# Retention, a gated feed-forward and eight experts on one core: two more weight sets made ahead, two more jobs in seven-block form

## The chip, the core and the metric

The kernel runs on one core of one Trainium2 chip, as one launch. The metric is the device time of that launch in microseconds (us). Of the kernel before there are three timed runs: 1972.39, 1973.30 and 1973.48 us, median 1973.3 us.

## The reference, cut to what matters

All arithmetic is fp32. With N = 2304 tokens, model width 512:

```
# 1 retention: 4 batches x 8 heads, 576 positions, head width 64
scores = (q @ k.T) / sqrt(64);  ret = scores * gamma[h] ** (i - j) for i >= j, else 0
x = (ret @ v), heads joined                                  # 2304 x 512
# 2 gated feed-forward, width 1536
xn = x / sqrt(mean(x*x, -1) + 1e-6) * rms_g
x  = (silu(xn @ w_gate) * (xn @ w_val)) @ w_out
# 3 eight experts, width 1024 each
logits = x @ w_gate2;  P = exp(logits - max)
8 times: P /= P.sum(1) + 1e-9;  P /= P.sum(0) + 1e-9;  P *= N / E
out = sum over e of P[:, e] * (relu(x @ w1[e]) @ w2[e])
```

## The kernel before, in words

**Numbers in two parts.** TensorE multiplies fp32 values as pairs: each operand is split into a high part (a cast, on ACT) and a low part (value minus high, on VectorE, called DVE here, or on GpSimd, called POOL), and a product is three matmuls, high x high, high x low and low x high.

**Gated sweeps.** The feed-forward runs in six sweeps (numbered 0 to 5 here), each over 256 of the 1536 columns and over five blocks of tokens (512, 512, 512, 384, 384). `gated_block` (L203 to L256) does one block of one sweep. For each of two column tiles it makes a gate and a value product (TensorE, tiles `gv`), takes silu (ACT, tile `t`), multiplies (DVE, L221), casts the high part (ACT, `ghi`, L226) and subtracts the low part (DVE, `glo`, L227). The two halves then go through `w_out` (TensorE, tiles `x`), and the four results are added to `acc` (DVE, L250). The code is written as generators. Each block has five steps, and the `x` products of a block stand in the third step of the next block, behind that block's first gate and value products.

After each step two helpers put their own instructions into the same queues. `step_weights` narrows the next sweep's weights from 64-bit words to fp32 and splits them (DVE L137 to L143 and L159). `late_steps`, the second, makes expert weights ahead of time. Its program is `late_weights` and `late_plan` (L721 to L764): a list `PREPARED` of weight sets is spread evenly over 125 steps, from the last two blocks of sweep 0 to the third block of sweep 5. One set is 128 x 1024 raw values of `w1` or of `w2` for one job. `prepared` (L679 to L718) turns it into seven split blocks, in five pieces of work at the step numbers p, p+1, p+2, p+4 and p+5 (`LATE_PLACES`): ACT casts, DVE subtracts and stores on SyncE's queue (SP); four subtractions on POOL (L708), which make the sums that seven-block products need; ACT casts again; DVE subtracts again, stores, and SP's request of the raw tile for the third set after this one (three raw tiles, `ahead_raw`, rotate).

**Jobs.** The experts run as 96 jobs: three units of 768 tokens, in each eight experts, in each four pairs of 128-wide column tiles. The first product, x @ w1, is in seven-block form everywhere: a 2 x 2 by 2 x 2 block product made with seven block products instead of eight, and with sums and differences of blocks. The second product, h @ w2, has two forms. In the first `LATE` jobs (0 to 11) `outputs_of` (L946) makes it plainly: six token tiles, 36 matmuls of 512 columns. The same jobs prepare their own weights (`first_weights`, `second_weights`) and store them in DRAM (`w1_kept`, `w2_kept`) for the units after. From job `LATE` on the second product is in seven-block form as well: 42 matmuls of 384 columns, one job later than its first product. Job `LATE` is called the opening job: it ends the plain form of the job before it and starts the new one, and its sums lie in borrowed tiles (`opening_homes`), one of them the buffer `prob_b1`. The weights of jobs 12 to 31 are the ones that the sweeps made ahead; `load_w1` (L976) and `load_w2` request them from DRAM.

**What sets the order.** Each engine runs its instructions in the order in which the Python code issues them, and so does SP's queue, where a request waits until its source or its target is free. There is no scheduler. Two more names: `keep_probs` (L981) transposes four token tiles of the routing probabilities on TensorE, copies them on ACT into the single buffer `xs`, and stores them in DRAM (`prob_kept`); `load_probs` brings an expert's row back, spread over all partitions. `finish_unit` (L1222) transposes a unit's sums on TensorE, one PSUM bank after another, and stores the output.

Of the kernel before, what the change touches and what calls it, by code (L numbers as in the profile page):

```python
# [19 lines left out]
NT = B * S  # L20
DM = H * D
# [25 lines left out]
NU = NT // UNIT  # L47
NCH = UNIT // 128
NPAIR = FE // 256
UJ = E * NPAIR  # L50
ROUTED = NPAIR + 2
LATE = 12
LATE_PLACES = (0, 1, 2, 4, 5)
W2_TURN = (2 - LATE) % 3
PREPARED = [(1, 0)] + [(n, which) for n in range(LATE, UJ) for which in range(2)]
# [4 lines left out]
def retention_glu_experts(ctx: ExitStack, tc: tile.TileContext, a, out):  # L60
# [916 lines left out]
    def load_w1(n):  # L977
        if n < len(jobs):
            nc.sync.dma_start(f32(w1_slots[n % 2]).rearrange("p a b c -> p (a b c)"), w1_kept[n % UJ])

    def keep_probs(i):  # L981
        ps = pac.tile([E, 512], F32, tag="ac", name=f"pt{i}")
        tiles = range(4 * i, min(4 * i + 4, TT))
        for c, t in enumerate(tiles):
            nc.tensor.transpose(ps[:, c * 128:(c + 1) * 128], prob[:, t, :], ident)
        size = len(tiles) * 128
        st = ev.tile([128, 2, T], F32, tag="xs", name=f"pts{i}").rearrange("p a b -> p (a b)")[:E, :size]
        nc.scalar.copy(st, ps[:, :size])
        nc.sync.dma_start(prob_kept[:, i * 512:i * 512 + size], st)
# [3 lines left out]
    def load_probs(n):  # L993
        if n < len(jobs):
            u, e, _ = jobs[n]
            nc.sync.dma_start(prob_b[(e - LATE // NPAIR) % 2], prob_kept[e, u * UNIT:(u + 1) * UNIT].partition_broadcast(128))

# [14 lines left out]
    for n, (u, e, g) in enumerate(jobs[:LATE]):  # L1012
# [87 lines left out]
            for _ in ys:  # L1100
                pass
        ys = outputs_of(n)
        if ROUTED < n <= ROUTED + -(-NT // 512):
            keep_probs(n - ROUTED - 1)
    for _ in seconds:
        pass

# [44 lines left out]
    def low(n, i, engine=None):  # L1152
        (hi, lo), x = operand(n, i)
        (engine or nc.vector).tensor_sub(lo, x, f32(hi))  # L1154
# [28 lines left out]
    def shared(n, j):  # L1183
        second(n, j, S1, T1, shared_sums[j], start=begins_sum(n))
# [60 lines left out]
    for n, (u, e, g) in list(enumerate(jobs))[LATE:]:  # L1245
        opening = n == LATE
        m, l = n - 1, n - 2
        pb = prob_b[(e - LATE // NPAIR) % 2]
        load_w1(n + 1)
        if u + 1 < NU and (e, g) == (E - 1, NPAIR - 3):  # L1250
            switch = unit_operands(u + 1)
        ahead = u + 1 < NU and (e, g) in ((E - 1, NPAIR - 3), (E - 1, NPAIR - 2))
        turn = u + 1 < NU and (e, g) == (E - 1, NPAIR - 1)
        begins = n % UJ == 0
        h_blocks, sums = opening_homes if opening else homes
        if g == NPAIR - 1:
            load_probs(n + 1)

        block_product(n, px, 0, "A11", start=True)
# [15 lines left out]
        if opening:  # L1275
            block_product(n, pv, 3, "S1", start=True)
            nc.scalar.copy(p5, pv)
            next(ys)
            block_product(n, py, 4, "S2")
            nc.scalar.copy(pz, py)  # L1280
            next(ys)
        else:
            low(m, S2)
            low(m, A12)
            if l < LATE:
                block_product(n, qz, 3, "S1", start=True)
            block_product(n, py, 4, "S2")
            nc.scalar.copy(pz, py)
            if turn:
                next(switch)  # L1290
            first(m, 0)
            high(m, S4)
            low(m, S3, nc.gpsimd)
            low(m, S4, nc.gpsimd)
            shared(m, 0)
            if l >= LATE:
                block_product(n, qz, 3, "S1", start=True)
            nc.scalar.copy(p5, qz)
            if ahead or begins:
                next(switch)  # L1300
            third(m, 0)
            c11(m, 0)
            add_11(m, 0)
            if l >= LATE and jobs[l][1:] == (E - 1, NPAIR - 1):
                add_shared(jobs[l][0], 1)
# [64 lines left out]
    n, l = len(jobs) - 1, len(jobs) - 2  # L1370
# [29 lines left out]
        ev.tile([128, 2, T], F32, tag="xs", name="st_xs").rearrange("p a b -> p (a b)"), old[:, 3].rearrange("p h t -> p (h t)"),  # L1400
        prob_b[0], o_first[:, 1, :], z.rearrange("p h t -> p (h t)"), prob_b[1],
    ]
    for _ in finish_unit(NU - 1, [shared_all, px_all, qx_all, py_all, qy_all, shared_1], [t[:, :DM] for t in stages]):
        pass


# [74 lines left out]
```

## Time and profile before

| what | value |
|---|---|
| median of three runs | 1973.3 us |
| the profiled execution, its own time | 1973.84 us |
| its span, first to last instruction | 1972.1 us |
| busy TensorE / DVE / ACT / POOL | 1959.8 / 1556.0 / 944.2 / 867.9 us |
| granted TensorE clock | 1.00 throughout |
| DMA | 515.48 MB, mean 261 GB/s |

"Busy" is the time in which at least one instruction of an engine ran. The end of a matmul is modelled, so matmuls overlap in the rows: the distance between two starts tells more of TensorE than the length of one. In a timeline row the first number is the start, the second the length, and a bracket gives the idle time of the engine before the row and what ended it. In a row of waits the numbers are the total, how often, and the longest. The sweeps with weights made ahead lie between 131 and 503 us, the jobs from 529.5 us to the end.

### The profile page before, as it was taken

How to read it: one execution, taken by the hardware profiler on the slowest of the kernel's cores; microseconds unless marked ns; L12 is line 12 of the kernel's file. 1: busy time of each engine (PE TensorE's matmuls, PEld its weight loads, DVE VectorE, ACT ScalarE, POOL GpSimd, SP SyncE). 2: the span in 40 equal slices, each digit the busy share in tenths (PEclk: the TensorE clock that was granted, in tenths of full speed). 3: DMA queues.
4: the chain of work that ended last, by engine and by line, in shares of the span. 5: the costliest groups of instructions: out<-in, count | busy, mean ns of one | idle time of the engine just before them, and what ended most of it. 6: DMA issues, size and time to landing. Idle time of an engine off the chain costs nothing.

```text
span 1972.1 us, 31400 instructions
## 1 busy us (share of the span) xinstructions
PE 1959.8 (99%) x11540; PEld 1864.8 (95%) x11540; DVE 1556.0 (79%) x2507; ACT 944.2 (48%) x1903; POOL 867.9 (44%) x805
## 2 busy tenths in 40 slices
PE   9999999999999999999999999999999999999998
PEld 8888988988889989999999999999999999999998
DVE  7869999886778776777797777777787777777777
ACT  4566555444454535444454444444445444444444
POOL 2204344343144424454574454444565544544543
PEclk9999999999999999999999999999999999999999
DMA  9428898887378887667678667676766776776763
GB/s 327 144 91 319 320 327 320 312 301 264 116 278 303 288 317 281 249 256 273 238 271 295 248 262 269 243 277 252 264 256 254 270 276 246 269 263 240 279 251 144
DMA packets 138154, 515.48 MB, mean 261 GB/s; under 512 B 14504, under 2 KB 37040, under 8 KB 120336
## 3 DMA queue, kind: packets, MB, share of 16 engines
q1 hardware_dynamic: 137328, 511.98, 70.4%
q8 instruction: 91, 1.49, 0.3%
q0 software_dynamic: 240, 0.79, 0.1%
q10 hardware_dynamic: 432, 0.70, 0.1%
q14 instruction: 63, 0.52, 0.1%
HBM read 390.40 MB, written 123.02 MB: 260 GB/s over the span
## 4 chain that ended last, share of the span: by engine, by line
PE 94%; DVE 3%; DMA 2%; ACT 1%; issue 0%; POOL 0%; ACTq 0%; SPq 0%; DVEq 0%; POOLq 0%
PE py L925 10%; PE pz L925 10%; PE px L925 10%; PE qx L1160 9%; PE qy L1160 9%; PE qz L1160 8%; PE gv L195 5%; PE gv L196 5%; PE gv L197 5%; PE qz L925 4%; PE x L196 2%; PE x L197 2%; PE x L195 2%; PE pv L1160 2%; PE e L1160 2%; PE y L197 2%
## 5 line engine op out<-in xcount | busy, mean ns | idle before, releaser
L1345 POOL TENSOR_TENSOR acc<-z,a_block 128x384 f32<-128x384 f32 x83 | 84.3, 1015 | 562.2 <-DVE z L1339 562.2
L708 POOL TENSOR_TENSOR ahead_raw<-ahead_raw 128x256 f32<-128x256 f32 x164 | 151.0, 921 | 245.3 <-DVE shared L692 95.2
L1154 DVE TENSOR_TENSOR xlo<-acc,xhi 128x384 fp32r<-128x384 f32 x250 | 235.5, 968 | 2.8 <-ACT xhi L1150 2.7
L1150 ACT CAST xhi<-acc 128x384 fp32r<-128x384 f32 x332 | 162.0, 513 | 91.7 <-POOL acc L1345 46.5
L1160 PE MATMUL qx<-xhi,w2c 128*128 128x384 f32 x502 | 167.8, 334 | 0.0
L1171 DVE TENSOR_TENSOR acc<-acc,qz 128x384 f32<-128x384 f32 x246 | 134.8, 548 | 25.9 <-PE qz L1160 25.9
L1189 ACT COPY qz<-qy 128x384 f32<-128x384 f32 x167 | 77.4, 463 | 139.7 <-PE qy L1160 132.0
L1181 ACT COPY qy<-qx 128x384 f32<-128x384 f32 x167 | 77.4, 463 | 123.6 <-PE qx L1160 116.3
L1154 POOL TENSOR_TENSOR xlo<-fifth,xhi 128x384 fp32r<-128x384 f32 x83 | 108.4, 1307 | 38.6 <-ACT xhi L1150 38.6
L1171 DVE TENSOR_TENSOR acc<-acc,qx 128x384 f32<-128x384 f32 x123 | 67.4, 548 | 71.0 <-PE qx L1160 71.0
L925 PE MATMUL py<-shared 128*128 128x384 f32 x576 | 115.9, 335 | 0.6 <-ACT py L1262 0.3
L925 PE MATMUL py<-shared,w1s 128*128 128x384 f32 x576 | 115.7, 335 | 0.0
L1160 PE MATMUL qz<-xhi,w2s 128*128 128x384 f32 x336 | 113.0, 336 | 0.1
L1160 PE MATMUL qz<-xhi,w_extra 128*128 128x384 f32 x332 | 111.6, 336 | 0.0
L1367 POOL TENSOR_TENSOR fifth<-acc 128x384 f32<-128x384 f32 x83 | 110.7, 1334 | 0.0
L1366 POOL TENSOR_TENSOR acc<-z 128x384 f32<-128x384 f32 x83 | 109.6, 1321 | 0.0
L925 PEld LDWEIGHTS py<-shared 128*128 128x128 f32 x576 | 101.2, 188 | 3.0 <-ACT py L1262 2.1
L925 PEld LDWEIGHTS py<-shared,w1s 128*128 128x128 f32 x576 | 101.2, 188 | 0.5
L1150 ACT CAST xhi<-a_block 128x384 fp32r<-128x384 f32 x84 | 43.2, 515 | 121.1 <-DVE a_block L1308 121.1
L925 PE MATMUL px<-xhi,w1s 128*128 128x384 f32 x320 | 94.5, 335 | 1.3 <-DMA w1s<-w_kept 1.3
L925 PE MATMUL px<-xhi,shared 128*128 128x384 f32 x320 | 94.7, 336 | 0.0
L1160 PEld LDWEIGHTS qx<-xhi,w2c 128*128 128x128 f32 x502 | 94.2, 188 | 0.0
(417 smaller groups left out, 6308.8 us busy)
## 6 DMA issues: line engine op xcount, KB each, us to landing
w1s<-w_kept SPq DMA_DIRECT2D x43, 1792.0 KB, 7.2
shared<-w_kept SPq DMA_DIRECT2D x42, 1792.0 KB, 7.1
w2s<-w_kept SPq DMA_DIRECT2D x42, 1024.0 KB, 7.0
w_extra<-w_kept SPq DMA_DIRECT2D x42, 768.0 KB, 6.6
w_kept<-shared SPq DMA_DIRECT2D x48, 512.0 KB, 4.8
w_kept<-wslots SPq DMA_DIRECT2D x44, 512.0 KB, 4.9
w2c<-w_kept SPq DMA_DIRECT2D x42, 512.0 KB, 7.7
w2c<-w_kept SPq DMA_DIRECT2D x84, 256.0 KB, 7.9
```

Of the source, the lines that this page charges most:

```text
L195: nc.tensor.matmul(ps, lhsT=lh, rhs=rh, start=start, stop=False)
L196: nc.tensor.matmul(ps, lhsT=lh, rhs=rl, start=False, stop=False)
L197: nc.tensor.matmul(ps, lhsT=ll, rhs=rh, start=False, stop=stop)
L708: nc.gpsimd.tensor_sub(w[:, o, :], w[:, x, :], w[:, y, :])
L925: nc.tensor.matmul(ps, lhsT=l, rhs=r[:, k, :], start=start and k == 0 and i == 0, stop=k == 1 and i == 2, skip_group_check=True,)
L1150: nc.scalar.copy(hi, x)
L1154: (engine or nc.vector).tensor_sub(lo, x, f32(hi))
L1160: nc.tensor.matmul(ps, lhsT=l, rhs=r, start=start and i == 0, stop=i == 2, skip_group_check=True)
L1171: nc.vector.tensor_add(dst, dst, ps)
L1345: nc.gpsimd.tensor_add(sums[0], z[:, 0, :], h_blocks[0])
L1366: nc.gpsimd.tensor_sub(sums[2], z[:, 1, :], z[:, 0, :])
L1367: nc.gpsimd.tensor_sub(sums[3], h_blocks[1], sums[1])
```

## The change

`LATE` goes from 12 to 10, so jobs 10 and 11 of the first unit take their second product in seven-block form, and job 10 is the opening job. The list `PREPARED` grows from 41 to 45 sets (w1 and w2 of jobs 10 and 11), over the same 125 steps. What else moves follows from that or stands beside it:

- The five calls of `keep_probs`, one each in jobs 7 to 11, become two in job 7, two in job 8 and one in job 9.
- The opening job's successor gets its w1 blocks by a request (`load_w1(LATE + 1)`) that stands ahead of the last stores of the job before, and no longer at the start of the opening job, behind them.
- `load_probs` of the next expert, where it falls into the job right after the opening job, stands behind the reads of the borrowed buffer.
- The last unit's six transposes take their banks in another order: the two that hold shared sums come last.

```
-LATE = 12
+LATE = 10
...
-        if ROUTED < n <= ROUTED + -(-NT // 512):
-            keep_probs(n - ROUTED - 1)
+        for i in range(2 * (n - ROUTED - 1), 2 * (n - ROUTED)):
+            if 0 <= i < -(-NT // 512):
+                keep_probs(i)
+    load_w1(LATE + 1)
     for _ in seconds:
         pass
...
-        load_w1(n + 1)
+        if not opening:
+            load_w1(n + 1)
...
-        if g == NPAIR - 1:
+        if g == NPAIR - 1 and l >= LATE:
             load_probs(n + 1)
...
             low(m, S4, nc.gpsimd)
+            if g == NPAIR - 1 and l < LATE:
+                load_probs(n + 1)
             shared(m, 0)
...
-    for _ in finish_unit(NU - 1, [shared_all, px_all, qx_all, py_all, qy_all, shared_1], [t[:, :DM] for t in stages]):
+    for _ in finish_unit(NU - 1, [px_all, qx_all, py_all, qy_all, shared_all, shared_1], [t[:, :DM] for t in stages]):
```

Three places show how instructions move. The first is DVE at the start of sweep 1, between two multiplications of the gated product. L692 is the low part of weights made ahead, L137 to L143 and L159 narrow the sweep's own weights, L221 and L227 belong to the gated product. Before:

```order
L692 TENSOR_TENSOR shared<-ahead_raw_1736,shared 128x2x256 x2
L221 TENSOR_TENSOR t_0_0_1999<-t_0_0_1999,gv_0_0_1_2006 128x512
L159 TENSOR_TENSOR wslots<-cv_1875,wslots 128x512
L137 TENSOR_SCALAR cv_2002<-cv_2002 128x512
L138 TENSOR_SCALAR cv_2002<-raw_1923 128x512
L139 SCALAR_TENSOR_TENSOR cv_2002<-cv_2002 128x512
L692 TENSOR_TENSOR shared<-ahead_raw_1735,shared 128x2x256
L692 TENSOR_TENSOR shared<-ahead_raw_1735,shared 128x256
L227 TENSOR_TENSOR glo_0_0_2059<-t_0_0_1999,ghi_0_0_2058 128x512
```

After:

```order
L692 TENSOR_TENSOR shared<-ahead_raw_1736,shared 128x2x256 x2
L692 TENSOR_TENSOR shared<-ahead_raw_1735,shared 128x2x256
L692 TENSOR_TENSOR shared<-ahead_raw_1735,shared 128x256
L221 TENSOR_TENSOR t_0_0_2001<-t_0_0_2001,gv_0_0_1_2010 128x512
L159 TENSOR_TENSOR wslots<-cv_1875,wslots 128x512
L137 TENSOR_SCALAR cv_2004<-cv_2004 128x512
L138 TENSOR_SCALAR cv_2004<-raw_1923 128x512
L139 SCALAR_TENSOR_TENSOR cv_2004<-cv_2004 128x512
L227 TENSOR_TENSOR glo_0_0_2063<-t_0_0_2001,ghi_0_0_2062 128x512
```

The fourth set's two first subtractions stand one step earlier; from here on the sets come closer together. Counted over the whole order, the L692 rows that stand ahead of the last `glo` of sweep 1 are 31 of 512 columns and 11 of 256 before, and 34 and 12 now; to the end of sweep 2, 56 and 20 before, 62 and 22 now; to the end of sweep 3, 82 and 28 before, 89 and 31 now; in all 123 and 41 before, 135 and 45 now.

The second place is SP's queue around the start of the opening job. L913 to L915 store w2 of the job before, L979 requests w1 blocks, L1140 (now L1142) w2 blocks. Before, with job 12 opening:

```order
L989 DMA prob_kept<-pts_7190 8x256
L913 DMA w_kept_1298<-xlo 128x4x512
L914 DMA w_kept_1298<-xlo 128x1024
L915 DMA w_kept_1298<-xlo 128x512
L979 DMA w1s_5548<-w_kept_1268 128x3584
L1140 DMA w2c_7199<-w_kept_1299 128x1024
```

After, with job 10 opening:

```order
L989 DMA prob_kept<-pts_7000 8x256
L979 DMA w1s_5616<-w_kept_1266 128x3584
L913 DMA w_kept_1296<-xlo 128x4x512
L914 DMA w_kept_1296<-xlo 128x1024
L915 DMA w_kept_1296<-xlo 128x512
L1142 DMA w2c_7010<-w_kept_1297 128x1024
```

The request of the next job's w1 blocks stands ahead of three stores instead of behind them.

The third place is the end of TensorE's program: the last matmuls of job 95, then six groups of four transposes. Before:

```order
L1160 MATMUL qz<-xhi,w_extra 128x384
L1226 MATMUL pv<-ident,acc 128x128 x4
L1226 MATMUL px<-ident,acc 128x128 x4
L1226 MATMUL qx<-ident,acc 128x128 x4
L1226 MATMUL py<-ident,acc 128x128 x4
L1226 MATMUL qy<-ident,acc 128x128 x4
```

After:

```order
L1162 MATMUL qz<-xhi,w_extra 128x384
L1228 MATMUL px<-ident,acc 128x128 x4
L1228 MATMUL qx<-ident,acc 128x128 x4
L1228 MATMUL py<-ident,acc 128x128 x4
L1228 MATMUL qy<-ident,acc 128x128 x4
L1228 MATMUL pv<-ident,acc 128x128 x4
```

The tile `pv`, which holds a shared sum that DVE reads late, comes fifth instead of first. The groups transpose the same parts of the output in the same order as before.

## Rows read from the trace of the kernel before

**Rows 1.** The page: busy us (share of the span) xinstructions of each engine.

```profile
PE 1959.8 (99%) x11540; PEld 1864.8 (95%) x11540; DVE 1556.0 (79%) x2507; ACT 944.2 (48%) x1903; POOL 867.9 (44%) x805
```

**Rows 2.** Windows, sweeps 1 to 3: busy PE, PEld, DVE, ACT, POOL; clock; DMA.

```profile
163.00:237.00 74.00, 73.85 (x359) 65.00 (x358) 68.77 (x108) 39.76 (x79) 31.47 (x32) 1.00 0.89 324
237.00:311.00 74.00, 74.00 (x361) 65.47 (x361) 69.02 (x112) 39.64 (x78) 33.08 (x36) 1.00 0.88 320
311.00:385.00 74.00, 74.00 (x361) 65.46 (x360) 64.38 (x106) 37.26 (x72) 28.22 (x33) 1.00 0.88 317
```

**Rows 3.** Waits of DVE, 163 to 311 us: total, times, longest.

```profile
DVE glo L227 <- ACT ghi L226: 9.5, 13, 1.2
```

**Rows 4.** Groups of DVE, 163 to 237 us: busy, mean ns | idle before.

```profile
L692 DVE TENSOR_TENSOR shared<-ahead_raw,shared 128x512 fp32r<-128x512 f32 x11 | 11.5, 1076 | 0.0
L692 DVE TENSOR_TENSOR wslots<-ahead_raw,wslots 128x512 fp32r<-128x512 f32 x13 | 11.3, 892 | 0.0
```

**Rows 5.** Groups of POOL, 163 to 459 us.

```profile
L708 POOL TENSOR_TENSOR ahead_raw<-ahead_raw 128x256 f32<-128x256 f32 x138 | 127.5, 924 | 172.5 <-DVE wslots L692 71.3 <-DVE shared L692 40.1 <-DVE w_more L692 23.2
```

**Rows 6.** Timeline of DVE in sweeps 1 and 2: start, length.

```profile
215.05 1.28 DVE L692 TENSOR_TENSOR wslots<-ahead_raw,wslots 128x512 fp32r<-128x512 f32 x2
...
231.45 2.37 DVE L692 TENSOR_TENSOR shared<-ahead_raw,shared 128x512 fp32r<-128x512 f32 x2
...
234.86 0.56 DVE L227 TENSOR_TENSOR glo<-t,ghi 128x384 fp32r<-128x384 f32 x1 [0.58 <-ACT ghi L226]
...
293.96 0.79 DVE L227 TENSOR_TENSOR glo<-t,ghi 128x384 fp32r<-128x384 f32 x1 [0.58 <-ACT ghi L226]
```

**Rows 7.** Timeline of PE, `x` products of sweeps 1 and 2.

```profile
234.96 0.36 PE L195 MATMUL x<-ghi,wslots 128*128 128x384 f32 x1
235.47 0.44 PE L196 MATMUL x<-glo,wslots 128*128 128x384 f32 x1
...
295.72 0.33 PE L195 MATMUL x<-ghi,shared 128*128 128x384 f32 x1
```

**Rows 8.** Waits of ACT, 163 to 385 us, the longest of raw tiles.

```profile
ACT wslots L687 <- DMA ahead_raw<-in_w_dram: 5.9, 3, 3.4
```

**Rows 9.** Timeline of PE: first matmul of jobs 11, 12, 13, 15 and 16.

```profile
704.72 0.42 PE L925 MATMUL px<-xhi,w1s 128*128 128x384 f32 x1
...
720.52 0.42 PE L925 MATMUL px<-xhi,shared 128*128 128x384 f32 x1
...
737.56 0.45 PE L925 MATMUL px<-xhi,w1s 128*128 128x384 f32 x1 [0.81 <-DMA w1s<-w_kept]
...
766.50 0.33 PE L925 MATMUL px<-xhi,w1s 128*128 128x384 f32 x1
...
781.06 0.33 PE L925 MATMUL px<-xhi,shared 128*128 128x384 f32 x1
```

**Rows 10.** Timeline of SP at the opening job: issue time, length.

```profile
721.34 0.28 SPq L989 DMA_DIRECT2D prob_kept<-pts  x1
...
727.23 1.24 SPq L979 DMA_DIRECT2D w1s<-w_kept  x1
```

**Rows 11.** Timeline around the first `keep_probs`, end of job 7.

```profile
656.28 0.60 PE L985 MATMUL pt<-ident,prob 128*8 128x128 f32 x4
...
657.52 0.34 SPq L989 DMA_DIRECT2D prob_kept<-pts  x1
...
662.95 1.23 PE L925 MATMUL py<-shared 128*128 128x384 f32 x6
```

**Rows 12.** Timeline of the kernel's end: DVE's last additions, PE's transposes.

```profile
1962.52 0.55 DVE L1171 TENSOR_TENSOR acc<-acc,qy 128x384 f32<-128x384 f32 x1
...
1964.05 0.66 PE L1226 MATMUL pv<-ident,acc 128*128 128x128 f32 x4 [1.35 <-DVE acc L1219]
...
1964.38 0.54 DVE L1171 TENSOR_TENSOR acc<-acc,qz 128x384 f32<-128x384 f32 x1
...
1965.42 0.60 PE L1226 MATMUL py<-ident,acc 128*128 128x128 f32 x4
```

## The prediction, made before the changed kernel ran

> **What bounds the kernel now.** I read the page's engine shares first. TensorE is busy for 1959.8 of 1972.1 us [rows 1] and its clock is granted in full, so the kernel is bound by TensorE's work from end to end. A change gains by taking matmuls out or by closing one of TensorE's few gaps, and loses by making TensorE wait. DVE's 79% is an average over stages, so I read it by sweep. In sweeps 1 and 2 DVE is busy for 68.8 and 69.0 of 74.0 us [rows 2]. The two leave 10.2 us of 148, and the waits view says what they are: 9.5 us in 13 waits of `glo` for ACT's cast [rows 3]. That wait is a turn-around of 0.6 to 0.7 us between DVE's multiplication and its subtraction. It does not shrink when DVE is late, because the cast starts when the multiplication ends. So DVE has no free time in sweeps 1 and 2, and it is where four more sets have to go. In sweep 3 it leaves 9.6 us, and after that more. The timelines give the margin to TensorE: at the end of sweep 1 `glo` ends at 235.42, and the matmul that reads it starts at 235.47, 0.51 us after the one ahead of it instead of 0.17 [rows 6, 7]. TensorE has waited there for 0.3 us already. In sweep 2 the closest `glo` ends at 294.75 and its reader starts at 295.72, a margin of 0.97 us [rows 6, 7].
>
> **The jobs.** Job 15 is in seven-block form and takes 781.06 - 766.50 = 14.56 us; job 11, a plain one, takes 720.52 - 704.72 = 15.80 us [rows 9]. Two transposes of the probabilities lie in the latter; four take 0.60 us with their modelled tail [rows 11], so two are some 0.25, and they are only moved to another job. That leaves 15.55, and 1.0 us a job for 36 matmuls of 512 columns against 42 of 384. The opening job and its two successors stay as they are, two jobs earlier. Two jobs: -2.0 us.
>
> **The request.** Job 13's first matmul waits for its w1 blocks: an idle time of 0.81 us that the DMA ends [rows 9]. The blocks were requested at 727.23, behind three stores that wait for DVE, and the entry ahead of those stores went out at 721.34 [rows 10]. The new place is right behind that entry, so the request goes out nearly 6 us sooner, more than the wait. Its slot is free by then, since the job before has ended its first product. The stores move back by one issue, and nothing near reads them. -0.8 us; the ends are 0, if DVE's subtractions for the second product are next in line, and -0.9.
>
> **The end.** The first transposes wait for bank `pv`, which DVE reads late, and start at 1964.05. What they transpose is complete when DVE ends `acc<-acc,qy` at 1963.07 [rows 12], so with `px` first they can start 0.9 us sooner. The fourth group needs `acc<-acc,qz`, done at 1964.92; it now starts at 1965.42 and could at 1964.97 [rows 12]. The last three groups, and the copies and stores behind them, move by that: -0.45 us.
>
> **`keep_probs` twice in a job.** The second copy on ACT needs the single buffer, so it waits for the first one's store, and behind it stands the copy of `px` that TensorE wants before its fourth block product. The store is issued at 657.52 and the product starts at 662.95 [rows 11], so there are 5.4 us for a small store and two copies. I take 0; if the store lands late, up to 1.5 us in the two jobs together. `load_probs` in job 11 is needed half a job later and is taken at 0 as well.
>
> **The sweeps.** Four sets more are 16 subtractions on DVE, 12 of 512 columns and 4 of 256, with 8 to 9 us of quiet work: two of 512 columns take 1.28 us by themselves and 2.37 us in other places [rows 6], so one costs 0.7 or 1.2 us. In sweep 1 the means are 1.08 and 0.89 us [rows 4], 0.98 over all 24. By the order three of 512 columns and one of 256 (taken at 0.42, half of 0.85) are added ahead of the last `glo` of sweep 1. DVE has no room, TensorE waits there already: 3 x 0.98 + 0.42 = 3.3 us, all on TensorE's path. That stall also clears DVE's backlog. In sweep 2 another 3.3 us is added; some 1.2 of it (one of each size, at a quieter mean) comes ahead of the point with 0.97 us of margin, and 0.3 us gets through. The rest is carried into sweep 3, whose 9.6 us are mostly waits for ACT, some of which close when DVE is late; there I take 1.0 us, between 0 and the 3 us that are carried in. From sweep 4 on there is room. Together 4.6 us. The low end is 0, if ends that now look tight give way; the high end is 12 x 0.98 + 4 x 0.42 = 13.4 us, if all of it shows up on TensorE.
>
> POOL makes 16 more subtractions of 0.92 us on average [rows 5], beside DVE. The slow pairs of rows 6 are those with POOL at work, and each of their instructions costs 0.55 us more than a quiet one. This price is in the means of rows 4 for the added instructions; for the other DVE work that the new POOL instructions meet, it is bounded by 16 x 0.55 = 8.8 us and is taken at 0, since POOL often waits for DVE itself [rows 5].
>
> The Trainium skill has a rule for this ("SBUF — State Buffer", section "Who interferes with whom"): a DVE instruction with two SBUF inputs and a GpSimd instruction that reads SBUF share a read port, and whichever comes second is blocked until the first is done. The trace agrees in kind: 1.2 us instead of 0.7. By the rule the block could be as long as the POOL instruction, 0.92 us, so 16 of them up to 14.7 us, which would make the slower rival below more likely and larger than 0.55 us each does.
>
> **The raw tiles.** Sets now begin every 117/44 = 2.66 steps instead of 117/40 = 2.93. From the request of a raw tile to its first use there were mostly 4 steps (three sets less five steps, rounded) and are now 3; a step is 74/25 = 3.0 us. ACT has waited for raw tiles up to 3.4 us [rows 8], and will wait oftener. While DVE is behind ACT, this is hidden by DVE's own lateness. I take 0 and keep up to 3 us for the range.
>
> **Sum.** -2.0 - 0.8 - 0.45 + 4.6 = +1.35 us. Made against the profiled execution (span 1972.1 us, own time 1973.84 us) that is 1975.2 us. This execution lies 0.5 us above the median of the three runs, which the change is carried over to: 1973.3 + 1.4 = 1974.7 us.
>
> **Rivals.**
>
> 1. DVE finds room, and the sweeps cost nothing. For it: rows 7 show one short stall only, and the subtractions move in step with the sets, so peaks may fall elsewhere. Against it: rows 2 and 3, by which the 148 us hold 0.7 us that are neither work nor turn-around. Time: 1973.3 - 3.25 = 1970.0 us.
> 2. DVE stays behind, and the kernel gets slower. The place is sweeps 1 to 3, where by the order 7 subtractions of 512 columns and 3 of 256 are added: 7 x 0.98 + 3 x 0.42 = 8.1 us. Each of the 10 POOL subtractions that come with 2.5 sets slows another DVE instruction by up to 0.55 us, half of them at least: 2.8 us. 10.9 - 3.25 = +7.6, so 1980.9 us. It decides as soon as `glo` is late at three or more blocks of sweeps 2 and 3, or more than 7.2 us of the sweeps' cost reach TensorE. For it: DVE's full sweeps. Against it: sweep 3's 9.6 us.
> 3. Raw tiles land too late, ACT stands still, and `silu` and `ghi` are late with it. For it: one step less. Against it: in sweeps 1 to 3 the waits in rows 8 made no stall of their own that I can find beside the one of rows 7. Three such waits of 3.4 us, half of each on TensorE's path, are 5 us: 1979.7 us with the DVE term, 1975.1 without.
> 4. The request doesn't do what it says, because stores or reads that are already on the way fill the DMA engines: 1975.5 us.
>
> **Chances.** Forecast 0.46, rival 1 0.24, rival 2 0.18, rival 3 0.08, rival 4 0.04. A difference of 0.2% (3.9 us) is about what a measurement of this kernel can tell from no change, so the bounds are 1969.4 and 1977.2 us. Faster takes the lower half of rival 1: 0.12. Slower takes rival 2, half of rival 3 and the forecast's upper end, where the sweeps cost over 7.2 us: 0.27. Within 0.2%: 0.61. The range runs from just under rival 1, 1969.6, to rival 2 at 1980.5, with about a tenth left out on each side; the forecast's own range, with the sweeps at 2.5 to 7 us, is 1972.5 to 1977.
>
> **What would show it.** Jobs 10 and on start 14.6 us apart, two jobs earlier. The opening job's successor starts without a wait for w1. `px` is transposed first, and the fourth group starts 0.05 us after DVE's last addition. In the sweeps, matmuls of `x` wait for `glo`: some 3 us at the end of sweep 1, less in sweeps 2 and 3, none later, and the windows of DVE in sweeps 1 and 2 show over 72 us of 77. If the sweeps end at the same time as before, the step on DVE's room is wrong; if they end over 7 us later, the price is. A wait for `py` at the start of jobs 8 and 9 would show `keep_probs` wrong.

## The result and the profile after

The kernel after takes 1988.1 us (median of six runs, 1984.5 to 1989.6), the kernel before 1973.2 us (six runs, 1972.4 to 1974.4). The ratio is 1.0071, 95% interval 1.0061 to 1.0082: slower by 0.7%, and outside the range that was forecast. The profiled execution of the kernel after is the quickest of its six (1984.52 us, span 1982.4 us); the trace explains its 10.3 us of span. The other five took up to 5.1 us more and left no trace.

Start with the first matmul of job 0, where the sweeps end. Before, it started at 529.54 us. This is TensorE's timeline after (start, length):

```profile
542.42 0.33 PE L925 MATMUL px<-xhi,shared 128*128 128x384 f32 x1
```

So the sweeps cost 12.88 us. From there everything is quicker: job 15 starts at 778.03, so job 0 to job 15 takes 235.61 us instead of 236.96 (-1.34), job 15 to job 95 takes the same within 0.1 us, and job 95 to the end of the span 31.94 instead of 33.23 us (-1.29). The four add up to the 10.3 us.

The windows by sweep (length; busy PE, PEld, DVE, ACT, POOL; clock; DMA share and GB/s) answer to [rows 2]. To hold the same work, each starts at the first gate product behind the last `x` products of the sweep before and ends at the same matmul a sweep later. Sweeps 1 to 3 before:

```profile
162.92:237.51 74.59, 74.44 (x361) 65.59 (x361) 69.36 (x109) 40.35 (x80) 31.47 (x32) 1.00 0.89 324
237.51:311.63 74.12, 74.12 (x361) 65.58 (x361) 69.14 (x112) 39.70 (x79) 33.08 (x36) 1.00 0.88 320
311.63:385.75 74.12, 74.12 (x361) 65.58 (x361) 64.50 (x104) 37.31 (x73) 28.89 (x34) 1.00 0.88 317
```

Sweeps 1 to 4 after:

```profile
162.04:238.95 76.91, 74.67 (x361) 65.55 (x361) 71.89 (x114) 44.44 (x87) 35.48 (x37) 1.00 0.96 347
238.95:321.15 82.20, 77.69 (x361) 66.85 (x361) 72.75 (x115) 40.20 (x79) 34.16 (x40) 0.98 0.87 313
321.15:398.16 77.01, 75.20 (x361) 65.50 (x361) 66.44 (x107) 39.27 (x77) 34.79 (x36) 1.00 0.87 318
398.16:472.28 74.12, 74.12 (x361) 65.58 (x361) 58.98 (x96) 33.98 (x66) 36.96 (x40) 1.00 0.94 335
```

Sweep 1 is 2.3 us longer, near the forecast; sweep 2 is 8.1 us longer, sweep 3 2.9 us, and sweep 4 takes its 74.12 us of before. The rest up to job 0 is 0.5 us longer. That is 13.8 us; 0.9 of it was made up ahead of sweep 1, before the first set is made, where the other runs differ by up to 1.1 us as well.

From DVE's side, sweep 1 has 2.5 us more work and no more idle time (5.0 us, before 5.2). In sweep 2 DVE has 3.6 us more work, and it is idle for 9.5 us of 82.2, where it was 5.0: it is late and has pauses too. ACT's waits in 163 to 395 us (total, times, longest) say what the pauses come from. They answer to [rows 8].

```profile
ACT wslots L687 <- DMA ahead_raw<-in_w_dram: 15.4, 5, 5.5
ACT shared L687 <- DMA ahead_raw<-in_w_dram: 14.7, 9, 2.8
ACT w_more L687 <- DMA ahead_raw<-in_w_dram: 9.5, 4, 4.9
```

Together 39.6 us in 18 waits for raw tiles; in the same window of the kernel before it is 15.4 us in 8. DVE's waits in that window show who waits behind ACT, and answer to [rows 3]:

```profile
DVE glo L227 <- ACT ghi L226: 21.1, 19, 4.6
DVE w_more L692 <- ACT w_more L687: 2.6, 1, 2.6
```

In the same window before, `glo` waited for 16.2 us in 20 waits, the longest 2.7. How one such wait becomes a stall is read from the timelines at the end of sweep 2 (start, length, and in brackets the idle time before and what ended it). ACT:

```profile
299.20 0.48 ACT L217 ACTIVATE t<-gv 128x384 f32<-128x384 f32 x1
304.57 0.93 ACT L687 CAST w_more<-ahead_raw 128x512 fp32r<-128x512 f32 x2 [4.90 <-DMA ahead_raw<-in_w_dram]
...
307.49 0.51 ACT L226 CAST ghi<-t 128x384 fp32r<-128x384 f32 x1
...
316.22 0.51 ACT L226 CAST ghi<-t 128x384 fp32r<-128x384 f32 x1 [2.09 <-DVE t L221]
```

DVE:

```profile
302.10 0.54 DVE L221 TENSOR_TENSOR t<-t,gv 128x384 f32<-128x384 f32 x1
305.23 1.03 DVE L692 TENSOR_TENSOR w_more<-ahead_raw,w_more 128x512 fp32r<-128x512 f32 x2 [2.58 <-ACT w_more L687]
308.03 1.09 DVE L227 TENSOR_TENSOR glo<-t,ghi 128x384 fp32r<-128x384 f32 x1 [1.78 <-ACT ghi L226]
309.04 1.93 DVE L250 TENSOR_TENSOR acc<-acc,x 128x384 f32<-128x384 f32 x4
...
313.31 0.41 DVE L137 TENSOR_SCALAR cv<-cv 128x512 f32<-128x512 f32 x1
...
315.64 0.55 DVE L221 TENSOR_TENSOR t<-t,gv 128x384 f32<-128x384 f32 x1
316.76 0.76 DVE L227 TENSOR_TENSOR glo<-t,ghi 128x384 fp32r<-128x384 f32 x1 [0.58 <-ACT ghi L226]
317.45 0.95 DVE L137 TENSOR_SCALAR cv<-cv 128x512 f32<-128x512 f32 x1
```

TensorE:

```profile
313.55 0.34 PE L197 MATMUL x<-ghi,shared 128*128 128x384 f32 x1
316.79 0.44 PE L195 MATMUL x<-ghi,shared 128*128 128x384 f32 x1 [2.90 <-ACT ghi L226]
```

DVE ends a multiplication at 302.64, but its cast `ghi` stands on ACT behind casts of a raw tile that lands only at 304.57, and starts at 307.49. DVE pauses twice, 2.58 and 1.78 us. TensorE goes on, since the products that read this `ghi` come only at 311.62. But from 308.03 to the next multiplication at 315.64 DVE works without a pause and doesn't catch up, so the next `ghi` comes at 316.22, and TensorE stands for 2.90 us, ten microseconds after ACT's wait is over. This one place holds 5.3 of sweep 2's 8.1 us.

The stall at the end of sweep 1 is another matter:

```profile
236.34 0.45 PE L195 MATMUL x<-ghi,wslots 128*128 128x384 f32 x1 [2.09 <-ACT ghi L226]
```

ACT waited for raw tiles ahead of it, for 3.18 us until 225.53 and for 1.91 us until 231.44. But there was a wait of 3.43 us until 224.86 before as well, and in both kernels DVE works from about 219 us to the end of its last multiplication in the sweep (235.74 us, before 234.28) without a pause. That stall comes from DVE's work and not from ACT's waits.

Behind the stall of sweep 2 TensorE pays once more. The windows, columns as above:

```profile
316.00:318.00 2.00, 0.86 (x2) 0.61 (x3) 1.42 (x3) 1.78 (x4) 1.84 (x3) 0.90 0.99 234
318.00:320.00 2.00, 2.00 (x8) 2.00 (x8) 1.97 (x4) 0.79 (x2) 0.91 (x2) 0.50 0.98 389
320.00:322.00 2.00, 2.00 (x9) 1.87 (x8) 2.00 (x4) 1.97 (x5) 0.00 (x0) 0.75 0.48 137
322.00:324.00 2.00, 2.00 (x11) 1.62 (x10) 2.00 (x5) 2.00 (x5) 0.00 (x0) 1.00 0.88 268
```

After 2.90 us of idleness the granted clock is at its lower level (0.50, 1.2 GHz) for some 3.4 us, to about 321 us, and matmuls of 384 columns start 0.32 us apart instead of 0.17: another 1.3 us. After the 2.09 us at the end of sweep 1 it stayed at 1.00:

```profile
234.00:236.00 2.00, 0.25 (x2) 0.00 (x0) 1.74 (x3) 0.22 (x1) 0.73 (x1) 1.00 0.92 289
236.00:238.00 2.00, 1.51 (x7) 1.25 (x8) 1.68 (x4) 2.00 (x5) 0.05 (x1) 1.00 1.08 389
```

Behind the sweeps two small waits of TensorE are new (whole span), and the opening job's 0.8 us for `w1s` [rows 9] is gone:

```profile
PE pt L985 <- ACT pts L988: 0.7, 1, 0.7
PE qx L1162 <- DMA w2c<-w_kept: 0.5, 1, 0.5
```

At the end, against [rows 12], TensorE's timeline:

```profile
1973.98 0.34 PE L1162 MATMUL qz<-xhi,w_extra 128*128 128x384 f32 x1
1974.16 0.38 PE L1228 MATMUL px<-ident,acc 128*128 128x128 f32 x2
...
1976.60 0.66 PE L1228 MATMUL qy<-ident,acc 128*128 128x128 f32 x4 [0.55 <-DVE acc L1173]
1977.09 0.60 PE L1228 MATMUL pv<-ident,acc 128*128 128x128 f32 x4
1977.53 0.60 PE L1228 MATMUL e<-ident,acc 128*128 128x128 f32 x4
```

The first transposes follow the last product with no wait, and the last group starts 3.55 us after the last product instead of 3.92.

### The profile page after: what moved, and what is told of

Read it like the earlier page. It is cut to its first block, busy times and chain, and to the rows that moved or that the text cites. A ratio compares the mean times of both kernels' runs of the same rounds, so it can differ in the third digit from the quotient of the medians.

```text
span 1982.4 us, 31556 instructions
## 1 busy us (share of the span) xinstructions
PE 1963.7 (99%) x11552; PEld 1867.0 (94%) x11552; DVE 1566.5 (79%) x2529; ACT 953.1 (48%) x1927; POOL 889.7 (45%) x817
## 4 chain that ended last, share of the span: by engine, by line
PE 82%; DVE 10%; DMA 4%; issue 2%; ACT 2%; SPq 0%; POOL 0%; DVEq 0%; ACTq 0%; POOLq 0%
PE py L925 10%; PE pz L925 10%; PE px L925 9%; PE qx L1162 9%; PE qy L1162 9%; PE qz L1162 9%; PE qz L925 4%; PE gv L195 2%; PE gv L196 2%; PE gv L197 2%; PE pv L1162 2%; PE e L1162 2%; DMA ahead_raw<-in_w_dram 2%; PE x L196 1%; PE x L197 1%
## 5 line engine op out<-in xcount | busy, mean ns | idle before, releaser
L708 POOL TENSOR_TENSOR ahead_raw<-ahead_raw 128x256 f32<-128x256 f32 x180 | 167.6, 931 | 242.4 <-DVE shared L692 100.6
L1156 DVE TENSOR_TENSOR xlo<-acc,xhi 128x384 fp32r<-128x384 f32 x256 | 240.9, 967 | 2.8 <-ACT xhi L1152 2.7
L1152 ACT CAST xhi<-acc 128x384 fp32r<-128x384 f32 x340 | 166.0, 513 | 94.1 <-POOL acc L1350 47.7
L1162 PE MATMUL qx<-xhi,w2c 128*128 128x384 f32 x514 | 171.8, 334 | 0.5 <-DMA w2c<-w_kept 0.5
```

The source lines that it names most:

```text
L708: nc.gpsimd.tensor_sub(w[:, o, :], w[:, x, :], w[:, y, :])
L1152: nc.scalar.copy(hi, x)
L1162: nc.tensor.matmul(ps, lhsT=l, rhs=r, start=start and i == 0, stop=i == 2, skip_group_check=True)
```

## The experiments

Theory A: DVE has no room in sweeps 1 to 3, partly because its instructions meet POOL's. Theory B: raw tiles land too late at the closer pace, ACT stands in its order, and `ghi` is late with it. Times are medians, ratios against runs of the kernel before on the same chip (medians 1973.3 to 1974.3 us). "Sweeps" is the start of job 0 against 529.54 us in the one execution that was profiled, "raw waits" ACT's waits for raw tiles in 163 to 395 us; for the kernel after these are +12.9 and 39.6 us.

**Sets alone, jobs alone.** The first makes four sets that nobody uses with the rest as before; the second makes 41 sets, and jobs 10 and 11 read the weights of jobs 14 and 15.

```
+PREPARED = [(1, 0)] + [(n, which) for n in range(LATE - 2, UJ) ...]   # before; two unused jobs' sets
```

> The kernel before (opening job 12, plain jobs 0 to 11, its own order of requests and transposes) with the four sets of jobs 10 and 11 made ahead as well, in the order and at the pace of the changed kernel, but stored where nobody reads them. If the sweeps alone hold the loss: job 0 starts 12 to 17 us later than in the kernel before and the time is 1985 to 1991 us. If the loss needs the new jobs: under 1978 us.

```
+PREPARED = [(1, 0)] + [(n, which) for n in range(LATE + 2, UJ) ...]   # after; jobs 10, 11 read w_kept of 14, 15
```

> The changed kernel, but its sweeps make only the 41 sets of the kernel before, at that pace; jobs 10 and 11 read the weights of jobs 14 and 15 instead, so their part of the result is another one. If the sweeps alone hold the loss: the sweeps end as in the kernel before and the time is 1973.2 less 2.6 us (what the changed kernel's jobs and end gained in its trace), 1970.6 us, within 1 us. By the terms of the prediction: 3.25 us less, 1969.9 us. If the new jobs carry a part of the loss: over 1974 us.

Measured: 1988.7 us, ratio 1.0077 [1.0062, 1.0092], sweeps +18.3, raw waits 49.8; and 1971.3 us, 0.9986 [0.9977, 0.9995], sweeps +0.5. All of the loss is in making the sets, and the rest of the change gains some 3 us.

**Relief of one suspect at the new pace.** First, no DVE subtractions in every eleventh set, so that DVE has the work of before:

```
+            if lows:                                   # lows = i % 11 != 5
                 nc.vector.tensor_sub(both[:, :, 1, :], blocks, f32(both[:, :, 0, :]))
```

> The changed kernel without VectorE's four subtractions in every eleventh set (4 of the 45, spread over sweeps 1 to 4); casts, GpSimd's subtractions, requests and stores of these sets stay, their low parts are not computed. VectorE's work in the sweeps is that of the kernel before, the pace of the raw tiles that of the changed kernel. Theory A, VectorE's full queue pays for each added subtraction: the stalls go, 1970 to 1973 us. Theory B, raw tiles land too late at the closer pace, ScalarE stands and the others behind it: most of the loss stays, 1979 to 1987 us.

Then the sets' later steps moved forward, which requests raw tiles sooner:

```
-LATE_PLACES = (0, 1, 2, 4, 5)
+LATE_PLACES = (0, 1, 1, 3, 4)
```

> The changed kernel with the five pieces of a set at steps 0, 1, 1, 3, 4 instead of 0, 1, 2, 4, 5: the same instructions, but a raw tile is requested one step sooner, so that there are 4 steps from request to use again, mostly, as in the kernel before. Theory A: VectorE's work is the same, 1983 to 1990 us. Theory B: ScalarE's waits for raw tiles fall from some 40 us in sweeps 1 to 3 to under 20, and at most the predicted 4.6 us stay in the sweeps: 1970 to 1976 us.

The first casts moved back instead:

```
+LATE_PLACES = (1, 1, 2, 4, 5)
...
-                put(at + place, (3, 1, 4, 2, 0)[step], i, step)
+                put(at + place, (1, 3, 4, 2, 0)[step], i, step)   # casts ahead of the step's subtraction
```

> The changed kernel with the first casts of each weight set one step later (places 1, 1, 2, 4, 5 instead of 0, 1, 2, 4, 5), so that a raw tile has 4 steps again, and the casts stand ahead of the step's subtraction; same sets, work and pace. Theory A expects 1987 to 1990 us, as the changed kernel. Theory B expects ScalarE's waits for raw tiles to fall from 39.6 us to under 15, TensorE's stalls to fall from 12 us to 4 or less, and 1972 to 1979 us. A third theory, C (the chain cast, subtraction, GpSimd's sums, cast, subtraction has no slack left at this pace, and whoever is first in it only hands the wait on), expects what the run with earlier places showed: the wait moves to VectorE (subtractions waiting for their casts) or to GpSimd's sums, and 1985 us or more.

Measured: 1986.3 us (1.0057 [1.0040, 1.0074]), sweeps +16.4; 1995.9 (1.0111 [1.0096, 1.0126]), +25.4; 1987.5 (1.0072 [1.0055, 1.0089]), +17.2. In the second ACT's raw waits are gone, and it waits for POOL's sums instead (14.9 and 11.7 us); in the third raw waits are down to 12.8 us, but ACT waits 31.0 us for DVE's `cv` (14.5 after). The wait only changes its place. Theory A as the amount of DVE's work fails in the first, theory B in its narrow form in the other two.

**A late tile at the old pace.** The kernel before with each raw tile requested one step later:

```
+            if i + 3 < len(PREPARED):
+                put(at + LATE_PLACES[4] + 1, -1, i, 5)      # step 5: load(i + 3)
```

> The kernel before with one thing changed: each raw tile is requested one step later, so that from request to first use there are 3 steps (mostly) instead of 4, as in the changed kernel; 41 sets, their pace, VectorE's and GpSimd's work stay. Theory A (VectorE has no room for more subtractions) expects no change, 1973 to 1975 us, job 0 at about 529.5. Theory B (raw tiles land too late, ScalarE stands in order and its casts ghi are late with it) expects ScalarE's waits for raw tiles, which were 14.7 us in 163 to 385 before, at 30 us or more, TensorE stalls of several us in the sweeps, and 1978 to 1988 us.

Measured: 1974.1 us, 1.0003 [0.9994, 1.0013], sweeps +0.5, raw waits 21.9 us. The three steps from request to use do no harm by themselves at the old pace. Theory B's expectation was wrong here, A's right. But the raw waits rose only from 15.4 to 21.9 us, so waits as long as the 39.6 us after are not tested by this run.

**Parts of the change without the sets.** The whole change at `LATE = 12`, and then the same with `keep_probs` once a job:

> The changed kernel with seven-block products from the thirteenth job on again: 41 sets and the sweeps of before, and of the change only the earlier request of the opening job's successor's weights, the pairing of keep_probs and the order of the last transposes. All theories expect the sweeps to be as before (job 0 at 529.5) and 1971.8 to 1973.0 us: 0.8 us less for the request, 0.45 us less at the end, 0 to 1 us more for keep_probs.

```
-        for i in range(2 * (n - ROUTED - 1), 2 * (n - ROUTED)):
-            if 0 <= i < -(-NT // 512):
-                keep_probs(i)
+        if ROUTED < n <= ROUTED + -(-NT // 512):
+            keep_probs(n - ROUTED - 1)
```

> The kernel before (41 sets, seven-block products from the thirteenth job on, one keep_probs a job) with only the earlier request of the successor's weights and the new order of the last transposes. All theories expect the sweeps as before, job 13 0.8 us earlier, the end 0.45 us earlier, and 1971.8 to 1972.4 us; if the run with both parts and keep_probs in pairs lost its gain to something else than the pairs, 1973 us or more.

Measured: 1973.8 us, 1.0003 [0.9994, 1.0013]; and 1971.9 us, 0.9989 [0.9980, 0.9998]. The pairs eat the gain, in jobs 7 to 9. Without them the request is worth 1.1 us (jobs 12 to 14), the end 1.0 us. The first kernel misses its expectation, by 0.8 us; the second meets it, and is quicker than the kernel before and the one after.

**Taking ScalarE, VectorE, the stores or GpSimd out of it.** ACT's first casts read resident data; one narrowing instruction of DVE left out; every second job's stores left out; POOL's sums left out.

```
+        high(0, other[:, 0:2, :]); high(1, other[:, 2:3, :])   # other: a part of xhi; ACT's casts only
```

> The changed kernel, but ScalarE's two first casts of each weight set read a resident part of the activations instead of the raw tile, so that ScalarE never waits for a raw tile; VectorE still subtracts from the raw tile, and sets, places, pace, GpSimd's sums and all transfers stay (the weights computed are not the reference's). Theory B (late raw tiles make ScalarE stand, and its casts ghi are late with it) expects ScalarE's 39.6 us of waits for raw tiles to go and the time to come back to 1971 to 1977 us. Theory A (VectorE has no room in sweeps 1 to 3, partly because its instructions meet GpSimd's more often) expects the waits to move to VectorE's subtractions and 1984 us or more.

```
-        nc.vector.tensor_scalar(size, size, LEAST, None, ALU.max)
```

> The changed kernel with one of VectorE's four narrowing instructions for each weight of the gated sweeps left out (the lower bound for zeros, line 137): 28 instructions, 18.2 us of VectorE in the sweeps of the changed kernel, more than the 16 added subtractions; all else stays. Theory A expects most of the loss to go, 1971 to 1977 us. Theory B expects ScalarE's waits for raw tiles to stay above 30 us, and 1983 us or more.

```
+        x[LATE + 1::2] = x[LATE::2]      # w1_kept, w2_kept; no stores for odd jobs
```

> The changed kernel without the stores of every second job's weight sets (later jobs read the neighbour's weights, so the output is not the reference's): about 40 MB less written in the sweeps, all work on the engines as it was. If full DMA engines (share 0.96 in sweep 1, 0.89 before) are what makes raw tiles late (theory D, a form of B), raw tiles land sooner, ScalarE's waits for them fall under 15 us and the time to 1971 to 1977 us. Theory A, and B with lateness from the request's place alone, expect 1984 us or more.

```
-        for o, x, y in signs:
-            nc.gpsimd.tensor_sub(w[:, o, :], w[:, x, :], w[:, y, :])
```

> The changed kernel with GpSimd's four subtractions of each weight set left out (the second casts read the raw blocks as they are; the weights are not the reference's). VectorE then meets no GpSimd instruction in the sweeps, which in the changed kernel made 21 of 56 instructions of lines 137 and 138 take 0.96 us instead of 0.42 (7 of 56 before), and the second casts do not wait for sums. Theory A expects VectorE's busy share to fall by a sixth and 1970 to 1974 us. Theory B expects raw tiles to be as late as they were and 1982 us or more.

Measured: casts 1982.8 us (1.0046 [1.0031, 1.0061]), sweeps +10.9, raw waits 0. Narrowing 1980.0 (1.0032 [1.0020, 1.0045]), +8.2, 45.4. Stores 1981.3 (1.0039 [1.0025, 1.0054]), +8.8, 18.6. Sums 1970.9 (0.9986 [0.9977, 0.9995]), -0.7, 53.7. The first three lie between the ranges of the theories, so neither theory is the whole. The casts are less clean than I meant: with no raw tile to wait for, ACT waits for the next thing, the stores that empty its staging slots (in 163 to 395 us):

```profile
ACT wslots L687 <- DMA w_kept<-wslots: 10.5, 9, 2.7
ACT shared L687 <- DMA w_kept<-shared: 8.2, 10, 1.8
ACT w_more L687 <- DMA w_kept<-w_more: 4.5, 5, 1.9
```

Together 23.2 us. Half the stores are the better test: these waits don't occur, raw waits are near the 15.4 us of before, DVE has all of its work, and 8.8 us of the loss stay. Full DMA engines are then a part of what makes the tiles late (theory D): with half the stores the DMA share in 163 to 395 us is 0.64 instead of 0.91, a raw tile lands 5.2 us after its issue instead of 6.3 (medians), and the raw waits halve. What shorter waits in SP's queue add to that was not separated, and the time that D expected did not come. With half the stores (columns as above), from 163 us to job 0,

```profile
163.00:538.34 375.34, 369.32 (x1788) 319.67 (x1787) 323.76 (x511) 188.65 (x366) 158.26 (x171) 1.00 0.56 194
```

DVE is busy for 323.8 us; in the kernel after it is 322.2 and before 312.1. The run without one narrowing instruction is the counterpart: DVE's work of before (312.4 us), long raw waits, and 8.2 us of loss. Without the sums things change. ACT's waits in 163 to 395 us, and the window:

```profile
ACT shared L687 <- DMA ahead_raw<-in_w_dram: 20.6, 9, 4.1
ACT wslots L687 <- DMA ahead_raw<-in_w_dram: 19.3, 8, 5.5
ACT w_more L687 <- DMA ahead_raw<-in_w_dram: 13.8, 5, 4.1
```

```profile
163.00:395.00 232.00, 232.00 (x1125) 204.69 (x1124) 187.31 (x345) 126.32 (x245) 0.00 (x0) 1.00 0.94 341
```

ACT waits longer for raw tiles than in the kernel after, and TensorE doesn't stand at all: DVE has 45 us of room and works every delay off. Theory B's 1982 us or more was wrong by 11 us.

**Contention or the chain.** Leaving the sums out removes the meetings of POOL and DVE, and the second casts' wait for the sums. Short sums keep that wait:

```
+            nc.gpsimd.tensor_sub(w[:, o, :64], w[:, x, :64], w[:, y, :64])
```

> The changed kernel with GpSimd's subtractions shortened from 256 to 64 columns a block (the rest of the blocks keeps the raw values, so the weights are not the reference's); their number, order and dependencies stay, and the second casts still wait for them. Without the sums at all the loss was gone, and that left two causes. If it is the meetings of GpSimd and VectorE in time (theory A with its price from GpSimd), a GpSimd instruction now takes a quarter to a half of 0.93 us, VectorE's slow instructions get rare or less slow, VectorE's work in 163 to 545 falls from 370 to about 345 us, and the time is 1970 to 1975 us. If it is the chain's wait for the sums, ScalarE and VectorE stand for them as before, and the time stays above 1980 us.

Measured: 1973.2 us, 0.9993 [0.9984, 1.0002], sweeps +3.2, raw waits 54.8. The window:

```profile
163.00:395.00 232.00, 229.09 (x1104) 200.85 (x1103) 187.14 (x338) 122.29 (x238) 53.60 (x112) 1.00 0.92 333
```

It is the meetings. The wait for the sums is kept, though a POOL instruction takes 0.48 us now; and in the kernel after it had been 0.2 us of ACT's time in this window, too little to be the loss. DVE's group of line 137 in 163 to 395 us (busy, mean ns) shows their price in the kernel before,

```profile
L137 DVE TENSOR_SCALAR cv<-cv 128x512 f32<-128x512 f32 x21 | 10.4, 495 | 0.4 <-ACT cv L135 0.4
```

after,

```profile
L137 DVE TENSOR_SCALAR cv<-cv 128x512 f32<-128x512 f32 x21 | 14.2, 676 | 0.0
```

and without sums:

```profile
L137 DVE TENSOR_SCALAR cv<-cv 128x512 f32<-128x512 f32 x21 | 8.8, 420 | 0.0
```

One such instruction takes 0.42 us alone and 0.95 beside POOL (the two rows of DVE above, 313.31 and 317.45). POOL's row around the second:

```profile
315.47 3.52 POOL L708 TENSOR_TENSOR ahead_raw<-ahead_raw 128x256 f32<-128x256 f32 x4 [5.75 <-DVE shared L692]
```

Over all DVE instructions of the sweeps the meetings come to some 41 us in both kernels, an estimate from busy times: 322.2 us after and 280.9 without sums; before 312.1, and 280.9 less the 9.8 us that the 16 added subtractions take without POOL (12 x 0.68 and 4 x 0.42, means of that run). The change has moved meetings from line 692 to lines 137 and 138, and not made more of them.

**Another spacing.** The same 45 sets, at the old pace first and faster later:

```
+            at = 2 + i * 117 // 40 if i < 18 else 51 + (i - 17) * 68 // 27
```

> The changed kernel with its 45 sets spaced otherwise: through sweeps 1 and 2, where VectorE is fullest, one set every 2.93 steps as before, and from there on one every 2.52 steps, so that the last set ends where it did. Theory A (the loss arises where VectorE has no slack to take up waits) expects sweeps 1 and 2 as before, some loss in sweep 3 (VectorE 64 of 74 us before, some 5 us more now) and none later: 1970 to 1976 us. Theory B (late raw tiles as such) expects stalls in sweeps 3 to 5, where there are now even less than 3 steps from request to use: 1980 us or more.

```
+            at = ... else 51 + (i - 17) * 25 // 9 if i < 27 else 76 + (i - 26) * 43 // 18
```

> As the run with another spacing, but sweep 3 at one set every 2.78 steps and sweeps 4 and 5 at one every 2.39. Theory A expects sweep 3 nearly as before and sweeps 4 and 5 (VectorE 59 of 74 us before, some 6 us more now) to hold it: 1970 to 1974 us. Theory B expects the raw tiles of sweeps 4 and 5 to be the latest of all and 1980 us or more.

Measured: 1988.8 us (1.0073 [1.0060, 1.0087]) and 1988.4 (1.0073 [1.0057, 1.0088]), sweeps +15.7 and +15.6. I set the change of pace too early: step 51 lies within sweep 2. Sweep 1 is as before in both (TensorE 73.85 of 74 us busy), and the first stalls of over 1 us, 3.06 and 2.63 us, come at 309 and 311 us, after the pace has risen. Sweep 3 loses 9.1 us in the first and 0.3 in the second, which is what A expected of it. But in the second the largest stall, 4.51 us, is in the last sweep, where raw tiles are late at 2.39 steps a set. Theory A's expectation of the time failed and theory B's came true: the late sweeps do not hold the faster pace. A cleaner split was not tried.

## Why the prediction was wrong

**What bounds the kernel** was right, and so was the first step on the sweeps: DVE has no free time in sweeps 1 and 2, and TensorE's stall at the end of sweep 1 came where it was put; the sweep got 2.3 us longer, against 3.3. (The range's upper end, 1980.5, is called rival 2; that rival's own sum is 1980.9 us. Nothing hangs on it.)

**The step that failed is the cost of late raw tiles in front of a full DVE.** The prediction took 0, since "While DVE is behind ACT, this is hidden by DVE's own lateness". In sweep 1 that held: ACT's raw waits rose from 5.7 to 12.6 us, and DVE's idle time stayed at 5 us. In sweep 2 it failed: DVE stood behind ACT for 4.5 us more than before, and with 72.8 us of work it couldn't win the time back. A second step failed beside it. The first stall, which "clears DVE's backlog", and the room in sweep 3 were to take up most of the added work, and 4.6 us were let through; but DVE's work in sweeps 1 to 3 grew by 8.1 us, the sum that rival 2 names, and all of it lengthened them.

The runs can be compared by the windows of sweeps 1 to 3 between the same matmuls (before: 222.8 us, DVE busy for 203.0). Added work is the growth of DVE's busy time, added pauses that of its idle time; the loss is their sum by the way they are made.

| run | raw waits | loss | added work | added pauses |
|---|---|---|---|---|
| kernel after | 39.6 | 13.3 | 8.1 | 5.2 |
| sets alone, unused | 49.8 | 18.4 | 9.7 | 8.7 |
| half the stores | 18.6 | 9.3 | 9.3 | 0.0 |
| no narrowing instruction | 45.4 | 9.0 | -0.5 | 9.5 |
| no subtractions in every eleventh set | 44.1 | 16.9 | 4.3 | 12.6 |
| casts from resident data | 0 | 11.1 | 7.5 | 3.6 |
| first casts moved back | 12.8 | 17.4 | 11.0 | 6.4 |
| later steps moved forward | 0 | 24.7 | 5.8 | 18.9 |
| short sums | 54.8 | 4.1 | -20.9 | 25.0 |
| no sums | 53.7 | -0.5 | -24.7 | 24.2 |

So there are two terms, and half the stores and no narrowing show each of them alone: some 9 us of work, or some 9 us of pauses. Together they are 13.3 us in the profiled execution of the kernel after, so they do not simply add. Up to the last block of sweep 2 that kernel and the one with half the stores lose the same 5.1 us; there the former loses 5.3 us and the latter 1.8. Pauses cost that only in front of a full DVE: with the sums out of the way DVE stands 24 to 25 us longer, and TensorE loses 4 us or nothing. The kernel after shows it too: in sweep 4 ACT's raw waits are 28.3 us, more than in any sweep ahead of it, DVE is busy for 59.0 us of 74.1, and nothing is lost.

Late raw tiles are only one thing that ACT can be late for. In the three runs of the table with raw waits of 0 or 12.8 us the loss is 11 to 25 us, with ACT waiting for stores, `cv` or sums instead. What is shown is that a late ACT costs time in front of a DVE without room, whatever ACT waits for; that the pauses of the kernel after belong to raw tiles rests on its timelines and on half the stores.

By sweep the loss is 2.3, 8.1, 2.9, 0.0 and 0.5 us, where I had 3.3, 0.3, 1.0 and 0. The median lies 3.6 us above the profiled execution; the nearest trace to those runs is that of the sets alone, with more of both terms. Rival 3 had the mechanism, at 5 us and a chance of 0.08; rival 2 had the full DVE, at +10.9 us before gains. It took both.

One run is not explained. With the subtractions of every eleventh set left out DVE has 314.9 us of work from 163 us to job 0, near the 312 of before, and yet its pauses grow by 12.6 us. My reading is that relief must come between a late tile and the next block's end, which four places out of 45 seldom do; that was argued and not tested.

**POOL's meetings** were "taken at 0" for the other DVE work, and that holds: some 41 us in both kernels. The rule of the Trainium skill ("SBUF — State Buffer", "Who interferes with whom") would have made the slower rival likelier. In kind the trace agrees: the subtractions of line 692, which have two inputs, take 0.68 us on average without the sums and 0.76 to 0.89 us with them after. But the kernel got slower without more meetings.

**TensorE's clock** was no term at all. A stall of some 3 us cost another 1.3 us.

**The jobs and the request** were forecast at -2.8 us up to job 15 and gave -1.34. Jobs 7 to 9 take 0.8 us more than moved transposes explain (0.7 us of it is the second group of transposes in job 8, which waits for ACT to copy the first one out of PSUM; the wait that the prediction named, of the second copy for the first one's store, is there with 2.8 and 2.6 us on ACT, and no product waits for it in this trace), and job 5 takes 0.3 more. Of the request's gain 0.5 us comes back as the wait for `w2c`, whose request stands behind the stores as before; in the three other runs with the early request that wait doesn't occur. The request alone, with 41 sets, gave 1.1 us, more than the 0.8 it was put at.

**The end** was put at -0.45 us. The last transposes gave 0.37, and the span's end came 1.3 us earlier; most of the other 0.9 lies behind the issue of the last store, which has 3.5 us to the end of the span instead of 4.2. In the three other runs with the new order job 95 and the end gained 1.0 us.

## What to carry to other kernels

A wait of an in-order engine isn't free because a busier engine is behind it: ask whether that engine has time to catch up before the next deadline, and price the two together. At 93% busy, the share that is left needs some 60 us to work off a delay of 4 us, an estimate from DVE's 71.9 of 76.9 us in sweep 1. Room can also be made on the full engine from outside: here POOL's short instructions, a test that leaves the sums incomplete, freed DVE of some 40 us and took most of the loss away, where 10 us less of DVE's own work took about a third.

## What the runs showed of the hardware

TensorE's granted clock fell to its lower level for some 3.4 us after an idle time of 2.90 us, in the middle of a kernel that ran at 1.00 before and after; behind an idle time of 2.09 us it stayed at 1.00. DVE's narrowing instructions of lines 137 and 138 take either some 0.42 or some 0.95 us and nothing between: of the 56 in the sweeps 22 took the longer time after (the expectation quoted above says 21) and 7 before. With POOL's instructions cut to 64 columns (0.48 us) the longer time is 0.54 to 0.55 us, in 17 of 56.
